# First attention steps in pairs: joint sums, reciprocals and split values, and a bank of its own for the second product

## The chip, the core and the metric

The kernel runs on one core of a Trainium2 chip. The core has five engines that run side by side, each in its own program order: TensorE (PE in the profile, with its weight loads as PEld), VectorE (DVE), ScalarE (ACT), GpSimd (POOL) and SyncE (SP), which issues most of the transfers. [...] TensorE writes into eight banks of PSUM; VectorE and ScalarE read from there. The metric is the device time of one execution in microseconds; it is 542.4 us before the change.

## The reference

Attention with a window, then two feed-forward blocks, condensed here. Only keys within 96 positions back, and the first 8, count:

```python
    scores = scale * np.matmul(q, k.transpose(0, 1, 3, 2))   # 2 x 8 heads, 768 x 768
    bias = -slopes[:, None, None] * dist[None, :, :]
    scores = np.where(keep, scores + bias, -1000000000.0)
    a = np.exp(scores - np.max(scores, axis=-1, keepdims=True))
    a = a / (np.sum(a, axis=-1, keepdims=True) + 1e-09)
    x = np.matmul(a, v)                       # then 1536 rows of 512
    h = x @ w_in                              # 512 -> 2048
    g = np.where(h > 0.0, h, np.exp(np.minimum(h, 0.0)) - 1.0)
    x = g @ w_out                             # 2048 -> 512
    return np.maximum(np.maximum(x @ w1, x @ w2), x @ w3) @ w_out2
```

## The kernel before

The attention is cut into 48 steps. A step is one block of 128 queries for one pair of heads; two steps in a row (even, odd) share one load of queries and keys and one of values, and four pairs make the eight heads of 256 rows. A block's key window has 232 columns (two chunks of 116), or 128 in the first block of a sequence, so of steps 0 to 7 the even ones are narrow and the odd ones wide, and steps 8 to 15 are all wide.

One step goes through the engines so:

- `scores_pe`: TensorE multiplies queries and keys of two heads (L228), into banks S0 and S1 for even steps, y0 and y1 for odd ones;
- `scores_dve`: VectorE adds the distances and takes the extreme of each row (L254), for one head and then the other;
- `scores_act`: ScalarE takes the exponential and its row sums (L275), twice; `sums` adds 1e-9 to the sums (L237);
- `recip` (L266) and `norm` (L288): VectorE divides;
- `turn_pe`: TensorE transposes the result (L298, L304), into one of three banks; `turn_act`: ScalarE copies it back (L315);
- `values_pe`: TensorE multiplies it with the values (L327), into the same bank; `values_high` (ScalarE, L337) and `values_low` (VectorE, L343) split that into two halves, `xh` and `xl`, which later products use.

The order is written by hand (`tc.manual_schedule`): each engine runs its instructions as the Python code emits them. The program's head, the loop over steps 0 to 15 in `windowed`, emits in turn k: scores of step k, transposes of step k-2, value products of step k-3, then the work on VectorE and ScalarE, ending with sums of k, reciprocal and normalisation of k-1 and the subtraction of k-4. Beside it the first weights are converted (`words`, from step 8 on: ScalarE L458 and L477, VectorE L462, L469 and L482) and idle TensorE time is filled with products that nobody reads (`FILL`, L765). The last two steps also emit the first half of the first block's first product (`f.product(h, ...)`, L677, 256 columns). `begin` and `run` follow: for the first 512 rows, 16 products `h` of the first layer, each followed by its activation (`elu_exp`, `elu_max`) and by its part of four output tiles `y` (`out_high` L708, `out_low` L716), with the other attention steps woven between. The remaining blocks and the second feed-forward block come after that.

Of the kernel before, what the change touches and what calls it, by code (L numbers as in the profile page):

```python
# [12 lines left out]
F32 = mybir.dt.float32  # L13
# [4 lines left out]
AF = mybir.ActivationFunctionType  # L18
ALU = mybir.AluOpType
# [18 lines left out]
GRP = 2 * P  # L38
# [78 lines left out]
class Windowed:  # L117
# [121 lines left out]
    def scores_dve(self, k, early=False, other=-1):  # L239
# [9 lines left out]
        p = pool.tile([P, 512], F32, tag=tag, name="p")  # L249
        m = self.sm.tile([P, 8], F32, tag="m", name="m", bufs=4)  # L250
        b0 = P if i else 0
        for u in range(2):
            o = slice(u * WIN, u * WIN + n)
            nc.vector.tensor_tensor_reduce(  # L254
                out=p[:, o], in0=sp[u], in1=self.base[:, b0:b0 + n],
                scale=2.0 ** -(2 * hp + u + 1) / UNIT, scalar=3e38,
                op0=ALU.add, op1=ALU.min, accum_out=m[:, u:u + 1],
            )
            if u == 0:
                self.recip(other)  # L260
        self.p_t[k] = p, m

    def recip(self, k):
        if k in self.p_t:
            m = self.p_t[k][1]
            self.nc.vector.reciprocal(m[:, 6:8], m[:, 4:6])  # L266

    def scores_act(self, k):
        if k >= len(self.steps):
            return  # L270
        n = self.geom(k)[-1]
        p, m = self.p_t[k]
        for u in range(2):
            o = slice(u * WIN, u * WIN + n)
            self.nc.scalar.activation(  # L275
                p[:, o], p[:, o], AF.Exp, bias=m[:, u:u + 1], scale=-1.0,
                accum_out=m[:, 2 + u:3 + u],
            )

    def norm(self, k):  # L280
        if k not in self.p_t:
            return
        nc = self.nc
        n = self.geom(k)[-1]
        p, m = self.p_t[k]
        for u in range(2):
            o = slice(u * WIN, u * WIN + n)
            nc.vector.tensor_scalar(p[:, o], p[:, o], m[:, 6 + u:7 + u], None, op0=ALU.mult)  # L288

    def turn_pe(self, k, tag="TX"):  # L290
        if k not in self.p_t:
            return
        nc = self.nc
        p, _ = self.p_t.pop(k)
# [104 lines left out]
class Feed:  # L399
# [304 lines left out]
    def out_high(self, y, fc, g, n):  # L704
        w = self.w[fc][:, 1]
        for e in range(NCC):
# [527 lines left out]
def windowed(tc, ctx, io, flag):  # L1234
    nc = tc.nc
    f = Feed(tc, ctx, io)
    own = ctx.enter_context(ExitStack())
    at = Windowed(tc, own, io, f.ps, f.xy, f.wt, f.act)
    at.close = own.close
    with tc.manual_schedule():  # L1240
# [9 lines left out]
        first = BLOCKS[0] // GRP * 8  # L1250
        x = f.split_tiles()
# [24 lines left out]
        for k in range(first):  # L1276
# [168 lines left out]
```

## Time and profile before

| | us |
|---|---|
| median of 3 runs (542.32 to 542.52) | 542.4 |
| the profiled execution, as timed | 542.16 |
| its span, first to last instruction | 540.4 |
| TensorE busy in the span | 530.4 |
| VectorE busy | 394.1 |
| ScalarE busy | 287.9 |

The profile is one execution. Its span leaves 1.76 us of the timed run outside. A line of the timeline is an instruction (or a run of alike ones, with their count) with start, duration, engine and line of the code, what it writes and reads, and, in brackets, for how long its engine stood idle before it and what ended that. Durations of neighbours on VectorE and ScalarE overlap a little. An fp32 product shows as two records, so that x8 is four products; the two heads of a step run side by side.

### The profile page before, as it was taken

Reading aid. Unit: us, or ns where it says so; the run is one execution under the profiler, and the core shown is the slowest. Engines: PE = TensorE matmul, PEld = TensorE weight load, DVE = VectorE, ACT = ScalarE, POOL = GpSimd, SP = SyncE. Lnnn points to the kernel's source line nnn. Section 1 sums busy time; section 2 is a strip of 40 time slices with the busy share of each in tenths; the row PEclk is TensorE's granted clock in tenths of the full one; section 3 lists DMA queues with packets and bytes.
Section 4 is the critical chain, followed back from the end, with each engine's and each line's share of the span. In section 5 each row is a group of like instructions: output and inputs, shape, how many; then the busy total and the mean of one; then the engine's idle time right before and its main releaser. Section 6 shows DMA issues by size and latency. Waiting matters only on the chain.

```text
span 540.4 us, 7753 instructions
## 1 busy us (share of the span) xinstructions
PE 530.4 (98%) x2746; PEld 427.0 (79%) x2746; DVE 394.1 (73%) x830; ACT 287.9 (53%) x650; POOL 82.9 (15%) x89
## 2 busy tenths in 40 slices
PE   8999999999999999999999999999999999999995
PEld 6667787777777888787888888788888888888884
DVE  6999999999845344443567657688886989779883
ACT  5989877888756555554645565551256321224120
POOL 4210000001000000000000044421035410335000
PEclk9999999999999999999999999999999999999999
DMA  8928255442210111000000031330028301776024
GB/s 295 384 93 329 106 194 196 156 161 84 101 44 24 45 44 44 21 19 1 0 2 0 5 118 35 116 131 26 1 87 301 138 1 45 272 287 234 1 81 159
DMA packets 23455, 59.21 MB, mean 110 GB/s; under 512 B 2416, under 2 KB 2416, under 8 KB 23408
## 3 DMA queue, kind: packets, MB, share of 16 engines
q1 hardware_dynamic: 18368, 49.46, 26.2%
q10 hardware_dynamic: 5040, 9.18, 4.5%
q8 instruction: 24, 0.39, 0.3%
q14 instruction: 23, 0.19, 0.1%
HBM read 49.19 MB, written 9.44 MB: 108 GB/s over the span
## 4 chain that ended last, share of the span: by engine, by line
PE 91%; DVE 4%; ACT 3%; DMA 1%; issue 0%; SPq 0%; DVEq 0%; ACTq 0%
PE h L677 26%; PE y L708 16%; PE y L716 8%; PE y L1027 8%; PE y L1121 5%; PE y L677 5%; PE S L1027 4%; PE TX L327 3%; PE TX L304 3%; PE S L228 2%; PE TX L1027 2%; PE S L1121 2%; PE S L677 2%; PE h L1027 2%; PE TX L1121 2%; ACT p L275 1%
## 5 line engine op out<-in xcount | busy, mean ns | idle before, releaser
L677 PE MATMUL h<-xh,w 128*128 128x512 f32 (+1 forms) x432 | 122.1, 387 | 0.1
L708 PE MATMUL y<-gh,w 128*128 128x512 f32 x384 | 98.8, 399 | 0.1
L513 POOL TENSOR_TENSOR w<-wr,w 128x512 fp32r<-128x512 f32 x42 | 62.9, 1508 | 232.6 <-ACT w L512 230.4
L677 PEld LDWEIGHTS h<-xh,w 128*128 128x128 f32 x432 | 80.2, 188 | 17.3 <-DVE e L702 0.6
L708 PEld LDWEIGHTS y<-gh,w 128*128 128x128 f32 x384 | 69.8, 188 | 14.5 <-issue 0.7
L677 PE MATMUL h<-xl,w 128*128 128x512 f32 (+1 forms) x216 | 71.0, 386 | 0.0
L702 DVE SCALAR_TENSOR_TENSOR e<-e,h 128x512 f32<-128x512 f32 x48 | 32.9, 686 | 50.0 <-ACT e L698 50.0
L512 ACT CAST w<-wr 128x512 fp32r<-128x512 f32 x42 | 27.5, 663 | 63.5 <-DVE wr L503 51.2
L697 ACT ACTIVATE e<-h 128x512 f32<-128x512 f32 x48 | 28.7, 598 | 55.7 <-PE h L677 50.9
L275 ACT ACTIVATE p<-p,m 128x232 f32<-128x232 f32 (+1 forms) x96 | 44.8, 470 | 17.5 <-DVE m L254 17.2
L716 PE MATMUL y<-gl,w 128*128 128x512 f32 x192 | 51.6, 391 | 0.0
L503 DVE SCALAR_TENSOR_TENSOR wr<-wr 128x512 uint32<-128x512 uint32 x48 | 44.3, 923 | 7.4 <-ACT wr L495 6.0
L689 DVE TENSOR_TENSOR gl<-e,gh 128x512 fp32r<-128x512 f32 x48 | 33.1, 690 | 19.9 <-ACT gh L684 19.9
L677 PEld LDWEIGHTS h<-xl,w 128*128 128x128 f32 x216 | 40.4, 188 | 8.1 <-issue 0.2
L198 POOL TENSOR_SCALAR raw<-raw,qsc 128x256 f32<-128x256 f32 x24 | 16.7, 698 | 192.3 <-DMA raw<-qk 178.4
L1027 PE MATMUL y<-t,w 128*128 128x512 f32 x180 | 42.7, 389 | 0.0
L716 PEld LDWEIGHTS y<-gl,w 128*128 128x128 f32 x192 | 36.0, 188 | 7.9 <-issue 0.3
L684 ACT CAST gh<-e 128x512 fp32r<-128x512 f32 x48 | 29.6, 617 | 23.5 <-DVE e L702 23.3
L469 DVE SCALAR_TENSOR_TENSOR wr<-wr 128x1024 uint32<-128x1024 uint32 (+1 forms) x37 | 40.2, 1098 | 0.6
L1027 PEld LDWEIGHTS y<-t,w 128*128 128x128 f32 x180 | 33.8, 188 | 7.0
L698 ACT ACTIVATE e<-e 128x512 f32<-128x512 f32 x48 | 30.3, 632 | 1.5
L1037 ACT CAST g<-m 128x512 fp32r<-128x512 f32 x18 | 10.9, 621 | 35.5 <-DVE m L1056 27.4
(155 smaller groups left out, 837.7 us busy)
## 6 DMA issues: line engine op xcount, KB each, us to landing
wr<-wa SPq DMA_DIRECT2D x14, 1024.0 KB, 6.9
wr<-wb SPq DMA_DIRECT2D x24, 512.0 KB, 4.7
v<-v SPq DMA_DIRECT2D x24, 256.0 KB, 2.8
part<-row ACTq DMA_DIRECT2D x24, 256.0 KB, 4.5
raw<-qk SPq DMA_DIRECT2D x16, 312.0 KB, 4.5
row<-part SPq DMA_DIRECT2D x12, 256.0 KB, 3.1
out<-rows ACTq DMA_DIRECT2D x11, 256.0 KB, 2.8
raw<-qk SPq DMA_DIRECT2D x8, 260.0 KB, 4.7
```

Of the source, the lines that this page charges most:

```text
L275: self.nc.scalar.activation(p[:, o], p[:, o], AF.Exp, bias=m[:, u:u + 1], scale=-1.0, accum_out=m[:, 2 + u:3 + u],)
L469: self.nc.vector.scalar_tensor_tensor(r[..., 0], r[..., 1], v, r[..., 0], op0=op, op1=ALU.bitwise_or)
L503: self.nc.vector.scalar_tensor_tensor(t, a, c, t, op0=op, op1=ALU.bitwise_or)
L513: nc.gpsimd.tensor_tensor(w[:, u, 1], v, w[:, u, 0].bitcast(F32), op=ALU.subtract)
L677: nc.tensor.matmul(out[:, o:n], w[:, part % 2, c * P:c * P + P], (xl if part == 2 else xh)[:, c, o:n], start=(c, part) == order[0], stop=( ...
L689: (engine or self.nc.vector).tensor_tensor(gl[:, 0:n], e[:, 0:n], gh[:, 0:n].bitcast(F32), op=ALU.subtract)
L698: self.nc.scalar.activation(e, e, AF.Exp, scale=-1.0)
L702: self.nc.vector.scalar_tensor_tensor(e, e, -1.0, h, op0=ALU.add, op1=ALU.max)
L708: self.nc.tensor.matmul(y[e][:, 0:n], w[:, a, e * P:e * P + P], g[0][:, 0:n], start=fc == 0 and a == 0, stop=False,)
L716: self.nc.tensor.matmul(y[e][:, 0:n], w[:, 0, e * P:e * P + P], g[1][:, 0:n], start=False, stop=fc == NFC - 1,)
L1027: self.nc.tensor.matmul(out, w[:, u, i % 2, b + c * P:b + c * P + P], o[:, i // 2, c], start=c == i == 0, stop=c == 1 and i == 2,)
L1121: nc.tensor.matmul(o, t[:, a, r], w[:, u, b], start=u == k == 0, stop=u == 1 and k == 2,)
```

## The change

Steps 0 to 13 are emitted in pairs. `sums` and `recip` take a count, and the two steps of a pair share one small tile `m`, so that one instruction serves four columns. The values of two steps go into one bank by `pair_pe`, and `pair_high` and `pair_low` split 256 columns at once. The transposes of a pair both stand in the odd turn: the even step's in bank y3, the odd step's in TX or y2 by turns, where the pair's values follow. Steps 6 and 11 take the buffer of tag `e`. Steps 14 and 15 are written out and go step by step, with the two halves of the first product (`part`) in their old number. The second product takes bank y3 and no longer bank h; the first outputs are issued for the first three output tiles, high and low, and then for the fourth.

```diff
-    def sums(self, k):
+    def sums(self, k, n=1):
         if k in self.p_t:
-            m = self.p_t[k][1]
-            self.nc.scalar.activation(m[:, 4:6], m[:, 2:4], AF.Copy, bias=1e-9)
+            _, m, c = self.p_t[k]
+            o = slice(c, c + 2 * n)
+            self.nc.scalar.activation(m[:, 2, o], m[:, 1, o], AF.Copy, bias=1e-9)
...
+    def recip(self, k, n=1):
         if k in self.p_t:
...
+            self.nc.vector.reciprocal(m[:, 3, o], m[:, 2, o])
...
+    def pair_high(self, k, x):
+        if k >= 0:
+            g, hp, _ = self.steps[k]
+            o = slice(g * GRP, g * GRP + GRP)
+            self.nc.scalar.copy(x[0][:, hp, o], self.t_t[k + 1][0][:, 0:GRP])
+
+    def pair_low(self, k, x):
+        if k >= 0:
+            g, hp, _ = self.steps[k]
+            o = slice(g * GRP, g * GRP + GRP)
+            self.t_t.pop(k)
+            self.nc.vector.tensor_tensor(
+                x[1][:, hp, o], self.t_t.pop(k + 1)[0][:, 0:GRP],
+                x[0][:, hp, o].bitcast(F32), op=ALU.subtract,
             )
...
-        h = self.ps.tile([P, 512], F32, tag="h", name="h")
+        h = self.ps.tile([P, 512], F32, tag="y3", name="h")
         self.product(h, self.w[1][:, 0], x, n, order=BEHIND)
...
-        self.out_high(y, 0, prev, n)
-        self.out_low(y, 0, prev, n)
+        for rows in range(NCC - 1), (NCC - 1,):
+            self.out_high(y, 0, prev, n, rows)
+            self.out_low(y, 0, prev, n, rows)
...
-            at.turn_pe(k - 2, tags[k % 3])
-            at.values_pe(k - 3)
-            if k >= first - 2:
-                f.product(h, f.w[0][:, 0], x, GRP, 0, (k - first + 2) * 6, 6)
-            at.scores_dve(k, True)
-            at.turn_act(k - 2, nc.scalar.copy)
-            at.scores_act(k)
-            at.values_high(k - 3, x)
-            at.sums(k)
-            at.recip(k - 1)
-            at.norm(k - 1)
-            at.values_low(k - 4, x)
...
+        for k in range(0, last, 2):
+            ahead(k)
+            at.pair_pe(k - 4)
+            at.scores_dve(k, True, spare=spare)
+            at.recip(k - 2, 2)
+            at.norm(k - 2)
+            at.norm(k - 1)
+            at.scores_act(k)
+            at.pair_high(k - 4, x)
+            behind(k)
+            k += 1
+            ahead(k)
+            at.turn_pe(k - 3, "y3")
+            at.turn_pe(k - 2, ("TX", "y2")[k // 2 % 2])
+            at.scores_dve(k, True, mates=mates, spare=spare)
+            at.scores_act(k)
+            at.sums(k - 1, 2)
+            at.turn_act(k - 3, nc.scalar.copy)
+            at.turn_act(k - 2, nc.scalar.copy)
+            at.pair_low(k - 5, x)
+            behind(k)
...
+        k = last
+        ahead(k)
+        at.pair_pe(k - 4)
+        part(0)
+        at.scores_dve(k, True)
+        at.recip(k - 2, 2)
+        at.norm(k - 2)
+        at.norm(k - 1)
+        at.turn_pe(k - 2, tags[k % 3])
+        at.scores_act(k)
+        at.pair_high(k - 4, x)
+        at.sums(k)
+        at.turn_act(k - 2, nc.scalar.copy)
+        at.pair_low(k - 4, x)
```

Here `ahead(k)` issues the loads and the scores of step k (and fills), `behind(k)` the next piece of weight conversion.

TensorE in the turns of steps 4 and 5, before (L228 scores, into S0/S1 for step 4 and y0/y1 for step 5; L298 and L304 transposes; L327 value products):

```order
L228 MATMUL S0_235<-raw_135 128x128
L228 MATMUL S1_236<-raw_135 128x128
L298 MATMUL y2_239<-ident_126,p_194 128x128 x2
L327 MATMUL TX_211<-p_169,v_146 64x128 x4
L228 MATMUL y0_259<-raw_135 128x232
L228 MATMUL y1_260<-raw_135 128x232
L304 MATMUL y3_263<-ident_126,p_218 116x128 x4
L327 MATMUL y2_239<-p_194,v_179 64x128 x2
```

And in the changed kernel, the same turns (its lines L309 and L315 are the transposes, L338 the value products):

```order
L228 MATMUL S0_224<-raw_135 128x128
L228 MATMUL S1_225<-raw_135 128x128
L338 MATMUL y2_206<-p_155,v_146 64x128 x2
L338 MATMUL y2_206<-p_168,v_146 64x128 x4
L228 MATMUL y0_246<-raw_135 128x232
L228 MATMUL y1_247<-raw_135 128x232
L309 MATMUL y3_250<-ident_126,p_186 128x128 x2
L315 MATMUL TX_253<-ident_126,p_211 116x128 x4
```

The value products of both steps of a pair have moved between the scores of step 4 and those of step 5, and the transposes of steps 2 and 3 behind the latter.

ScalarE in the turns of steps 4 and 5, before (L275 exponentials, L237 sums, L315 copies of the transposes, L337 the split):

```order
L315 COPY p_194<-y2_239 128x256
L275 ACTIVATE p_246,m_247<-p_246,m_247 128x128 x2
L337 CAST xh_143<-TX_211 128x128
L237 ACTIVATE m_247<-m_247 128x2
L315 COPY p_218<-y3_263 116x512
L275 ACTIVATE p_270,m_271<-p_270,m_271 128x232 x2
L337 CAST xh_143<-y2_239 128x128
L237 ACTIVATE m_271<-m_271 128x2
```

And in the changed kernel (L284, L239, L326 and L364):

```order
L284 ACTIVATE p_234,m_235<-p_234,m_235 128x128 x2
L364 CAST xh_143<-y2_206 128x256
L284 ACTIVATE p_258,m_235<-p_258,m_235 128x232 x2
L239 ACTIVATE m_235<-m_235 128x4
L326 COPY p_186<-y3_250 128x256
L326 COPY p_211<-TX_253 116x512
```

Both copies of a pair now stand behind the pair's one sum.

TensorE in the turns of steps 14 and 15, before (L677 is the first product; S0/S1 belong to step 14, y0/y1 to step 15):

```order
L228 MATMUL S0_542<-raw_340 128x232
L228 MATMUL S1_543<-raw_340 128x232
L304 MATMUL y3_546<-ident_126,p_491 116x128 x4
L327 MATMUL y2_512<-p_454,v_403 64x128 x4
L677 MATMUL h_145<-xh_143,w_467 128x256 x6
L228 MATMUL y0_574<-raw_340 128x232
L228 MATMUL y1_575<-raw_340 128x232
L304 MATMUL TX_578<-ident_126,p_521 116x128 x4
L327 MATMUL y3_546<-p_491,v_470 64x128 x4
```

And in the changed kernel (L705 is the first product):

```order
L228 MATMUL S0_504<-raw_319 128x232
L228 MATMUL S1_505<-raw_319 128x232
L338 MATMUL TX_482<-p_395,v_377 64x128 x4
L338 MATMUL TX_482<-p_425,v_377 64x128 x4
L705 MATMUL h_145<-xh_143,w_434 128x256 x6
L315 MATMUL y3_531<-ident_126,p_457 116x128 x4
L228 MATMUL y0_542<-raw_319 128x232
L228 MATMUL y1_543<-raw_319 128x232
L315 MATMUL TX_546<-ident_126,p_487 116x128 x4
L338 MATMUL y3_531<-p_457,v_437 64x128 x4
```

The transposes of step 12 (before: y3, first in the row after the scores) have moved behind the values of steps 10 and 11 and the six products.

## Rows read from the trace of the kernel before

**Rows 1.** The page: busy time by engine, and the chain that ended last by engine

```profile
PE 530.4 (98%) x2746; PEld 427.0 (79%) x2746; DVE 394.1 (73%) x830; ACT 287.9 (53%) x650; POOL 82.9 (15%) x89
...
PE 91%; DVE 4%; ACT 3%; DMA 1%; issue 0%; SPq 0%; DVEq 0%; ACTq 0%
```

**Rows 2.** Busy time by stretch: us from:to, length, engines, TensorE clock, transfers

```profile
6.00:20.00 14.00, 12.52 (x104) 7.90 (x102) 11.50 (x65) 12.31 (x55) 3.14 (x7) 1.00 1.03 396
20.00:33.00 13.00, 11.91 (x102) 8.21 (x99) 12.82 (x47) 12.50 (x43) 3.09 (x5) 1.00 0.78 279
33.00:45.00 12.00, 11.91 (x108) 8.97 (x106) 10.47 (x42) 10.49 (x35) 1.02 (x1) 1.00 0.44 167
45.00:150.00 105.00, 104.85 (x588) 82.88 (x587) 99.17 (x210) 84.69 (x187) 6.31 (x7) 1.00 0.43 154
```

**Rows 3.** The chain that ended last, in order of time: start, us, what

```profile
10.70 0.95 ACT p L275 x4
...
12.73 0.21 DVE xl L343
...
14.32 0.95 ACT p L275 x4
...
17.94 0.95 ACT p L275 x4
```

**Rows 4.** Timeline of steps 0 to 3, ScalarE and VectorE: start, us, engine, what

```profile
6.88 0.39 ACT L275 ACTIVATE p<-p,m 128x128 f32<-128x128 f32 x1
...
7.50 0.47 ACT L275 ACTIVATE p<-p,m 128x232 f32<-128x232 f32 x1
...
7.82 0.48 DVE L288 TENSOR_SCALAR p<-p,m 128x128 f32<-128x128 f32 x2
...
8.56 0.20 ACT L237 ACTIVATE m<-m 128x2 f32<-128x2 f32 x1
...
8.72 0.37 ACT L315 COPY p<-y 128x256 f32<-128x256 f32 x1
8.80 0.17 DVE L266 RECIPROCAL m<-m 128x2 f32<-128x2 f32 x1
...
9.00 0.59 DVE L288 TENSOR_SCALAR p<-p,m 128x232 f32<-128x232 f32 x2
...
9.51 0.39 DVE L254 CUSTOM_DVE_ANT_0 p<-y,rel 128x232 f32<-128x232 f32 x1
...
10.60 0.49 ACT L275 ACTIVATE p<-p,m 128x232 f32<-128x232 f32 x1
```

**Rows 5.** Timeline of steps 5 to 8, TensorE and the reduce that waits for it

```profile
13.63 0.44 PE L327 MATMUL y<-p,v 128*64 128x128 f32 x4
...
14.95 0.66 PE L327 MATMUL y<-p,v 116*64 116x128 f32 x8
...
15.53 0.66 PE L228 MATMUL y<-raw 64*128 64x232 f32 x4
...
17.62 0.66 PE L228 MATMUL S<-raw 64*128 64x232 f32 x4
...
18.31 0.40 DVE L254 CUSTOM_DVE_ANT_0 p<-S,rel 128x232 f32<-128x232 f32 x1 [0.33 <-PE S L228]
```

**Rows 6.** Timeline of the last steps, and the second product's first weight load

```profile
32.54 1.23 DVE L469 SCALAR_TENSOR_TENSOR wr<-wr 128x1024 uint32<-128x1024 uint32 x1
...
33.69 0.39 DVE L254 CUSTOM_DVE_ANT_0 p<-S,rel 128x232 f32<-128x232 f32 x1
...
33.91 0.98 PE L677 MATMUL h<-xh,w 128*128 128x256 f32 x6
...
35.45 0.62 PE L304 MATMUL TX<-ident,p 128*116 128x128 f32 x4
...
36.11 0.58 ACT L315 COPY p<-TX 116x512 f32<-116x512 f32 x1 [0.68 <-PE TX L304]
...
45.36 0.19 PEld L677 LDWEIGHTS h<-xh,w 128*128 128x128 f32 x1 [0.35 <-DVE e L702]
```

More of the change, by code (lines that the diff above doesn't have):

```diff
@@ L232, in scores_pe, with scores_dve @@
             self.s_t[s] = [x[:, o:o + n] for x in sp]
-    def sums(self, k):
+    def sums(self, k, n=1):
         if k in self.p_t:
-            m = self.p_t[k][1]
-            self.nc.scalar.activation(m[:, 4:6], m[:, 2:4], AF.Copy, bias=1e-9)
-    def scores_dve(self, k, early=False, other=-1):
+            _, m, c = self.p_t[k]
+            o = slice(c, c + 2 * n)
+            self.nc.scalar.activation(m[:, 2, o], m[:, 1, o], AF.Copy, bias=1e-9)
+    def scores_dve(self, k, early=False, other=-1, mates=(), spare=()):
         if k not in self.s_t:
@@ L248, in scores_dve @@
         pool, tag = (self.act, "gh") if early and k % 4 > 1 else (self.sm, "p")
-        p = pool.tile([P, 512], F32, tag=tag, name="p")
-        m = self.sm.tile([P, 8], F32, tag="m", name="m", bufs=4)
+        if k in spare:
+            p = self.act.tile([P, 512], F32, tag="e", name="p", bufs=1)
+        else:
+            p = pool.tile([P, 512], F32, tag=tag, name="p")
+        if k - 1 in mates:
+            m, c = self.p_t[k - 1][1], 2
+        else:
+            m, c = self.sm.tile([P, 4, 4], F32, tag="m", name="m", bufs=4), 0
         b0 = P if i else 0
@@ L256, in scores_dve @@
                 scale=2.0 ** -(2 * hp + u + 1) / UNIT, scalar=3e38,
-                op0=ALU.add, op1=ALU.min, accum_out=m[:, u:u + 1],
+                op0=ALU.add, op1=ALU.min, accum_out=m[:, 0, c + u:c + u + 1],
             )
@@ L260, in scores_dve @@
                 self.recip(other)
-        self.p_t[k] = p, m
-    def recip(self, k):
+        self.p_t[k] = p, m, c
+    def recip(self, k, n=1):
         if k in self.p_t:
-            m = self.p_t[k][1]
-            self.nc.vector.reciprocal(m[:, 6:8], m[:, 4:6])
+            _, m, c = self.p_t[k]
+            o = slice(c, c + 2 * n)
+            self.nc.vector.reciprocal(m[:, 3, o], m[:, 2, o])
     def scores_act(self, k):
@@ L271, in scores_act @@
         n = self.geom(k)[-1]
-        p, m = self.p_t[k]
+        p, m, c = self.p_t[k]
         for u in range(2):
@@ L275, in scores_act @@
             self.nc.scalar.activation(
-                p[:, o], p[:, o], AF.Exp, bias=m[:, u:u + 1], scale=-1.0,
-                accum_out=m[:, 2 + u:3 + u],
+                p[:, o], p[:, o], AF.Exp, bias=m[:, 0, c + u:c + u + 1], scale=-1.0,
+                accum_out=m[:, 1, c + u:c + u + 1],
             )
@@ L284, in norm @@
         n = self.geom(k)[-1]
-        p, m = self.p_t[k]
+        p, m, c = self.p_t[k]
         for u in range(2):
             o = slice(u * WIN, u * WIN + n)
-            nc.vector.tensor_scalar(p[:, o], p[:, o], m[:, 6 + u:7 + u], None, op0=ALU.mult)
+            nc.vector.tensor_scalar(
+                p[:, o], p[:, o], m[:, 3, c + u:c + u + 1], None, op0=ALU.mult
+            )
     def turn_pe(self, k, tag="TX"):
@@ L293, in turn_pe @@
         nc = self.nc
-        p, _ = self.p_t.pop(k)
+        p = self.p_t.pop(k)[0]
         tp = self.ps.tile([P, 512], F32, tag=tag, name=tag)
@@ L345, in values_low @@
                 x[0][:, hp, o:o + P].bitcast(F32), op=ALU.subtract,
+            )
+    def pair_high(self, k, x):
[11 more added lines that the diff above has]
+                x[0][:, hp, o].bitcast(F32), op=ALU.subtract,
             )
@@ L702, in elu_max, with out_high @@
         self.nc.vector.scalar_tensor_tensor(e, e, -1.0, h, op0=ALU.add, op1=ALU.max)
-    def out_high(self, y, fc, g, n):
+    def out_high(self, y, fc, g, n, rows=range(NCC)):
         w = self.w[fc][:, 1]
-        for e in range(NCC):
+        for e in rows:
             for a in range(2):
@@ L711, in out_high, with out_low @@
                 )
-    def out_low(self, y, fc, g, n):
+    def out_low(self, y, fc, g, n, rows=range(NCC)):
         w = self.w[fc][:, 1]
-        for e in range(NCC):
+        for e in rows:
             self.nc.tensor.matmul(
@@ L1275, in windowed, with ahead @@
         tags = "TX", "y2", "y3"
-        for k in range(first):
+        last = first - 2
+        mates, spare = range(0, last, 2), (6, 11)
+        def ahead(k):
             e = k % 2
@@ L1284, in windowed, with behind @@
                 f.fill(at.ident, FILL[k])
-            at.turn_pe(k - 2, tags[k % 3])
-            at.values_pe(k - 3)
-            if k >= first - 2:
-                f.product(h, f.w[0][:, 0], x, GRP, 0, (k - first + 2) * 6, 6)
-            at.scores_dve(k, True)
-            at.turn_act(k - 2, nc.scalar.copy)
-            at.scores_act(k)
-            at.values_high(k - 3, x)
-            at.sums(k)
-            at.recip(k - 1)
-            at.norm(k - 1)
-            at.values_low(k - 4, x)
+        def behind(k):
             if k >= CONV:
@@ L1300, in windowed, with part @@
                 f.w_load()
+        for k in range(0, last, 2):
[19 more added lines that the diff above has]
+            behind(k)
+        def part(n):
+            f.product(h, f.w[0][:, 0], x, GRP, 0, n * 6, 6)
+        k = last
[12 more added lines that the diff above has]
+        at.pair_low(k - 4, x)
+        behind(k)
+        k += 1
+        ahead(k)
+        at.turn_pe(k - 2, tags[k % 3])
+        at.values_pe(k - 3)
+        part(1)
+        at.scores_dve(k, True)
+        at.turn_act(k - 2, nc.scalar.copy)
+        at.scores_act(k)
+        at.values_high(k - 3, x)
+        at.sums(k)
+        at.recip(k - 1)
+        at.norm(k - 1)
+        behind(k)
         def half(first, count):
```

## The prediction

> **What bounds the kernel now.** I read the page first: TensorE is busy for 98% of the span and holds 91% of the chain that ended last [rows 1]. By that, little can be won. But the share is an average, so I next cut the span into stretches [rows 2]. From 45 us on TensorE is busy for 104.85 of 105 us: whatever comes late there ends late, one to one. Before 45 us it is another program, the first 16 attention steps. From 6 to 20 us ScalarE is busy for 88% and VectorE for 82%; neither is full, so a loop of waits sets the pace. From 20 to 33 us VectorE is busy for 12.82 of 13 us: it is the bound. From 33 to 45 us both stand idle for 1.5 us, and the hand-overs decide again. The change edits these three stretches, and each has its own price.
>
> I use short names: S(k) the score products of step k, X(k) its reduce on VectorE (L254), E(k) its two exponentials, T(k) the transposes, C(k) their copy by ScalarE, V(k) the value products.
>
> The chain of waits shows the loop of 6 to 20 us [rows 3]: E of an odd step starts at 10.70, 14.32 and 17.94, so a pair of steps takes 3.62 us. Between two of them stand normalisation, subtraction, T, C. TensorE only steps in with T; S and V are not on the loop.
>
> **The change, part by part.** The order of instructions shows that it does what it says: sums, reciprocals and split values are issued once for two steps, and T of both steps stands behind S of the odd step. Times below are set against the profiled run (540.4 us span, 542.16 us as timed, 0.24 under the median).
>
> *Start.* The sum between E(0) and E(1) goes, so E(1) starts when E(0) lets ScalarE go, 6.88 + 0.39 = 7.27 and not 7.50 [rows 4]. From E(1) to its sum are 8.56 - 7.50 = 1.06 us, to the reciprocal 0.24, to the normalisation 0.20. That of step 0 holds VectorE for 0.40 (0.48 less the 0.08 by which 9.00 + 0.59 passes 9.51), that of step 1 for 0.51. X(3) then takes 0.40 and hands over in 0.02. E(3) starts at 7.27 + 1.06 + 0.24 + 0.20 + 0.40 + 0.51 + 0.42 = 10.10, where it is 10.60 now: 0.50 earlier.
>
> *The loop, steps 3 to 7.* In the new order TensorE has, in one queue, S(even), V of the pair two back, S(odd), T, T. V needs the copies C, and C now stand behind the joint sum on ScalarE. So S(odd) waits behind V, V behind C, C behind the sum, the sum behind E(odd), and E(odd) behind X(odd), which needs S(odd): a closed loop. Its length: sum 0.12 (0.20 less 0.08 overlap), C of 256 columns 0.29 (0.37 less 0.08), C of 512 columns 0.58 [rows 4, 6], hand-over 0.05 (estimate; 17.62 + 0.66 to 18.31 is 0.03 [rows 5]), V 0.80, S to X 0.69, X to E 0.42, E to sum 1.06. V: two products take 0.44, four 0.66, so six 0.88, and the next group starts 0.08 before their end (15.53 against 14.95 + 0.66); S to X is 17.62 to 18.31, a start on which VectorE waited [rows 5]. Sum: 4.01 us, 0.39 over today's 3.62. Two turns cost 0.78, so E(7) starts at 10.10 + 8.02 = 18.12 and not at 17.84.
>
> *Into the second stretch.* X(8) needs S(8), which now stands behind S(7), T(6), T(7). S(7) started at 18.12 - 0.42 - 0.69 = 17.01; then 0.58, 0.33 (two transposes, between nothing and the 0.54 of four, put at four less the value products' step of 0.11 each), 0.54 and 0.69: X(8) at 19.15 and not at 18.31 [rows 5, 6]. **+0.84.**
>
> *VectorE-bound, X(8) to X(14).* Three pairs each lose one reciprocal (0.20, 8.80 to 9.00) and have one subtraction of 256 columns for two of 128 (0.21 each [rows 3]). No row has the wide one: it costs between 0.21 and 0.42, I take 0.32. So 0.30 a pair, 0.20 to 0.41. **-0.90** (0.6 to 1.2). X(14) then comes within 0.1 us of today's 33.69.
>
> *The way out, X(14) to C(13).* Today C(13) starts at 36.11, 2.42 after X(14) [rows 6]. In the new order T(12) and T(13) wait for a normalisation issued only after X(14), and on TensorE they stand behind V(10), V(11) and six products of the first block (and T(13) behind S(15) too). V(10) needs the copies behind the joint sum: from X(13) 0.42 + 1.06 + 0.12 + 0.50 + 0.58 + 0.05 = 2.73, while X(14) stands at X(13) + 0.64 + 0.32 + 1.15 (two heads, the subtraction, the weight conversion of 32.54 to 33.69) = 2.11. So V starts 0.62 after X(14). Then V 1.02, the six products 0.90 (0.98 less 0.08), T(12) 0.54, S(15) 0.58, T(13) 0.62 and 0.04 to the copy: 4.32. Against 2.42 that is **+1.90**. From C(13) on ScalarE has the same order in both kernels, so nothing there earns it back unless idle time takes it up.
>
> *Second product's bank.* The second product has its own bank, so it no longer waits for the activation to be read from the first's: TensorE's weight load stood idle for 0.35 before it [rows 6]. About 0.05 of that is the usual switch. **-0.30**, between 0 and -0.35. The first outputs by rows put the one that reuses this bank behind nine products of the others; I cost it at nothing because these nine cover the activation's read of that bank, and at up to 0.3, the size of the wait removed, if that read is late. The removed instructions on ScalarE (one sum per pair, 0.12) cost and bring nothing of their own where the loop above decides. Transfers keep their order on SyncE; a load that waits for V to free its buffer moves with V, by under 1 us, and is used four pairs later, which covers that. The spare buffers of steps 6 and 11 cost nothing: the pair's V, ahead of X in time, frees the others.
>
> Sum: 0.84 - 0.90 + 1.90 - 0.30 = **+1.54 us**. On the profiled run 543.7, on the median 542.4 + 1.5 = **543.9**. Ends of the unknown terms: 0.84 - 0.2 - 1.2 + 1.8 - 0.35 = +0.9, and 0.84 + 0.2 - 0.6 + 2.0 = +2.4: 543.3 to 544.8 for this case.
>
> **Rivals.**
> A, *the joint work pays, faster.* The loop closes through V only because TensorE gets to X(odd) late. Copies end 0.99 after the sum starts, and S(odd) has delivered 0.05 + 0.80 + 0.69 later, at 2.53; VectorE is ready for X(odd) at 0.24 + 0.20 + 0.40 + 0.51 = 1.35. If V and S took under 0.36 us instead of 1.49, ScalarE's own work would set the turn: E 4 x 0.39 to 0.47, some 1.72, copies 0.87, the split 0.29, the sum 0.12: 3.00. Two turns then save 2.0, and V(10), V(11) out of the way of T(12) another 1.02: 1.54 - 3.02 = -1.48, **540.9**. For it speaks VectorE's full stretch; against it the V and S rows, four times too long. [...]
>
> B, *idle time takes up the late copy.* From 33 to 45 us ScalarE stands idle for 12 - 10.49 = 1.51 us [rows 2]. If the 1.90 ate all of it, the sum is about 0: **542.4**. Against it: ScalarE's idle is spent waiting for T, which come late by the same amount.
>
> C, *TensorE's clock falls.* TensorE was granted full clock in every stretch while busy for 89% from 6 to 20 us [rows 2]. In the new loop its groups hold 0.58 + 0.80 + 0.58 + 0.33 + 0.54 = 2.83 of 4.01 us, 71%, with one idle piece of over 1 us a turn. Were the clock to fall to its lower level, V and S on the loop (1.49) would at most double: 3.0 for two turns, **546.9**. [...]
>
> **How the numbers follow.** Forecast 0.72, A 0.08, B 0.12, C 0.08. The range must leave out no more than A and C: from B with 0.2 of room, 542.2, to just above the forecast's upper end, 545.0. About 0.2% (1.08 us) is what a measurement of this kernel can tell from no change. A is faster: 0.08. B, and the 0.10 of the forecast that lies under 543.5, are the same: 0.22. The rest of the forecast and C are slower: 0.70.
>
> **What would show it.** In the changed kernel's trace: E of steps 3, 5 and 7 about 4.0 us apart, the first at 10.1; X(odd) waiting for TensorE; V starting right behind a 512-column copy and S(odd) right behind V. X(8) to X(14) in about 14.5 us, where it is 15.38. C(13) more than 4 us after X(14). The first 512-column product near 46.9, where it is 45.36, with no wait on the activation. The forecast is wrong if the turns are 3.6 us or less, or if C(13) follows X(14) within 3 us; a granted clock under 1.00 before 45 us would mean C.

## The result, and the profile after

The changed kernel takes **546.4 us** (median of six, 544.4 to 546.9) against 542.5 us (542.2 to 542.6): a ratio of 1.0066, 95% interval 1.0056 to 1.0077. It is slower, by 3.9 us in the medians (3.6 in the means, from which the ratio comes), where the forecast was +1.5 us and the range ended at 545.0. Two slow executions of the kernel before, at 660.9 and 1065.7 us, count in none of the numbers below.

The profiled execution took 546.78 us with a span of 544.8 us. The first thing to look at is the clock column of the stretches, which answers to [rows 2]. Busy time by stretch in the changed kernel (from:to, length, then TensorE, its weight loads, VectorE, ScalarE, GpSimd, then TensorE's granted clock, transfers, GB/s):

```profile
10.00:15.00 5.00, 3.47 (x30) 2.58 (x30) 3.25 (x19) 3.52 (x13) 0.87 (x2) 0.90 1.03 407
15.00:20.00 5.00, 4.53 (x27) 3.00 (x26) 2.35 (x13) 2.96 (x13) 0.96 (x2) 0.50 1.04 397
20.00:25.00 5.00, 5.00 (x40) 3.58 (x40) 4.06 (x19) 4.97 (x16) 0.47 (x1) 0.92 0.69 229
```

In the kernel before, the clock is 1.00 from 6 to 150 us. Here it is 0.50 from 15 to 20 us, a level that the trace of the kernel before shows only behind its last product (at 533.8), from 537.9 us on; the single instructions put the low stretch at 13.7 to 20.6 us. TensorE looks busier in it (4.53 of 5 us) because its instructions take longer (V 1.55 us instead of 0.88, below). That was rival C.

The chain of the changed kernel, which answers to [rows 3], shows a turn of the loop on either side of the fall (start, length, what):

```profile
10.48 1.06 ACT p L284 x4
...
12.57 0.88 PE y L338 x12
13.45 0.64 PE y L228 x4
14.63 1.06 ACT p L284 x4
...
16.71 1.55 PE TX L338 x12
18.26 1.08 PE y L228 x4
```

V (L338) and S of the odd step (L228) now lie on the chain, which they did not before. The turn E(3) to E(5) takes 14.63 - 10.48 = 4.15 us. In the next one V takes 1.55 instead of 0.88 and S 1.08 instead of 0.64, and E(7) comes 5.29 us after E(5).

The timeline has the four places on which the rest hangs: the first value products of a pair, X(8), X(14) and C(13). They answer to [rows 5, 6]:

```profile
12.57 0.88 PE L338 MATMUL y<-p,v 128*64 128x128 f32 x12 [1.53 <-ACT p L326]
...
21.45 0.40 DVE L262 CUSTOM_DVE_ANT_0 p<-S,rel 128x232 f32<-128x232 f32 x1 [0.90 <-PE S L228]
...
36.02 0.40 DVE L262 CUSTOM_DVE_ANT_0 p<-S,rel 128x232 f32<-128x232 f32 x1
...
40.38 0.58 ACT L326 COPY p<-TX 116x512 f32<-116x512 f32 x1 [0.59 <-PE TX L315]
```

The first row is the pause: TensorE stood still for 1.53 us until the second copy C was done, and 1.15 us later its clock fell. X(8) is 3.14 us later than before (18.31), X(14) 2.33 us later (33.69), C(13) 4.27 us later (36.11). Of each, 0.37 us is a later X(0) (6.51 against 6.14), a scatter that the last section takes up. From there on the distance changes little: the second block's first product is 4.1 us later (56.90 against 52.78) and the last product of the kernel 4.5 us (538.3 against 533.8); what adds the last 0.4 us was not followed up.

The weight loads of the second product and of the first outputs (the bracket is idle time and what ended it):

```profile
49.27 0.19 PEld L705 LDWEIGHTS h<-xh,w 128*128 128x128 f32 x1
...
55.50 0.30 PEld L736 LDWEIGHTS y<-gh,w 128*128 128x128 f32 x2 [0.34 <-DVE e L730]
```

The wait of 0.35 us ahead of the second product [rows 6] is gone, and a wait of 0.34 us on the same kind of read now stands ahead of the fourth output row.

### The profile page after: what moved, and what is told of

Same layout as the page of the kernel before. It is cut to its first block, busy times and chain, and to the rows that moved or that the text cites. A ratio compares the mean times of both kernels' runs of the same rounds, so it can differ in the third digit from the quotient of the medians.

```text
span 544.8 us, 7720 instructions
## 1 busy us (share of the span) xinstructions
PE 532.7 (98%) x2746; PEld 429.3 (79%) x2746; DVE 392.8 (72%) x817; ACT 287.8 (53%) x637; POOL 81.6 (15%) x89
## 4 chain that ended last, share of the span: by engine, by line
PE 92%; ACT 3%; DVE 3%; DMA 1%; issue 1%; SPq 0%; ACTq 0%; DVEq 0%
PE h L705 27%; PE y L736 16%; PE y L744 8%; PE y L1056 7%; PE y L1150 4%; PE y L705 4%; PE S L1056 4%; PE TX L338 3%; PE TX L315 3%; PE S L228 3%; PE S L1150 2%; PE TX L1056 2%; PE S L705 2%; PE h L1056 2%; PE TX L1150 1%; ACT p L284 1%
## 5 line engine op out<-in xcount | busy, mean ns | idle before, releaser
L705 PE MATMUL h<-xh,w 128*128 128x512 f32 (+1 forms) x432 | 122.2, 387 | 0.0
L705 PEld LDWEIGHTS h<-xh,w 128*128 128x128 f32 x432 | 80.1, 188 | 17.4 <-issue 0.5
L705 PE MATMUL h<-xl,w 128*128 128x512 f32 (+1 forms) x216 | 71.0, 386 | 0.0
L284 ACT ACTIVATE p<-p,m 128x232 f32<-128x232 f32 (+1 forms) x96 | 44.8, 470 | 21.8 <-DVE m L262 21.7
L705 PEld LDWEIGHTS h<-xl,w 128*128 128x128 f32 x216 | 40.4, 188 | 8.2 <-issue 0.2
```

The source lines that it names most:

```text
L284: self.nc.scalar.activation(p[:, o], p[:, o], AF.Exp, bias=m[:, 0, c + u:c + u + 1], scale=-1.0, accum_out=m[:, 1, c + u:c + u + 1],)
L705: nc.tensor.matmul(out[:, o:n], w[:, part % 2, c * P:c * P + P], (xl if part == 2 else xh)[:, c, o:n], start=(c, part) == order[0], stop=( ...
```

## The experiments

All are compared with the kernel before on the same chip, whose median was 542.3 to 542.6 us. e1, e2, e3 and e5 ran on one chip, e4, e6, e7 and e8 on a second, e9 to e11 on a third, so that across these groups the ratio is the better comparison.

| label | edit | median us | ratio to before, 95% |
|---|---|---|---|
| e8_after | the changed kernel again | 545.6 | 1.0057 (1.0044 to 1.0069) |
| e1_fills | more empty products at three pauses | 544.6 | 1.0039 (1.0025 to 1.0052) |
| e7_one_piece | more empty products at one pause | 544.7 | 1.0040 (1.0027 to 1.0053) |
| e6_nofill | before, without its empty products | 543.1 | 1.0021 (1.0003 to 1.0038) |
| e3_loop | e1, V later in two turns | 543.7 | 1.0023 (1.0013 to 1.0033) |
| e4_out | e1, pairs for steps 0 to 7 only | 543.7 | 1.0024 (1.0015 to 1.0034) |
| e5_loop_out | both of these | 542.5 | 1.0004 (0.9994 to 1.0013) |
| e9_tail | e1, T(12) and T(13) ahead | 544.4 | 1.0036 (1.0023 to 1.0050) |
| e10_late_all | e1, V later in all turns | 547.3 | 1.0089 (1.0073 to 1.0104) |
| e2_bank | before, with the bank and the rows | 542.3 | 0.9999 (0.9990 to 1.0008) |
| e11_no_rows | e2 without the rows | 543.1 | 1.0018 (1.0009 to 1.0027) |

### The clock: e1, e8, e7

The kernel has a table FILL of empty products (L793), which work on nothing that is used later. e1 adds some at the pauses of the paired loop:

```diff
-FILL = {1: 2, 2: 2, 8: 2, 9: 2, 10: 2, 11: 2, 12: 2, 13: 2}
+FILL = {1: 2, 2: 4, 4: 4, 6: 4, 8: 2, 9: 2, 10: 2, 11: 2, 12: 2, 13: 2}
```

> The changed kernel, with the empty products of L793 raised where TensorE idles in the paired loop: 4 instead of 2 behind S(2), and 4 new ones each behind S(4) and S(6). Nothing else differs. Theory 1 (the lower TensorE clock costs about 2.0 to 2.4 us of the loss, on top of a loss of 1.5 to 2 us by the order alone): the granted clock is 1.00 in 10:15, 15:20 and 20:25, the turn E(5) to E(7) falls from 5.29 to about 4.1 us, and the time is 544.3 us (543.8 to 544.8). Theory 2 (the clock comes out of the loop's stalls and is not their cause; the loss is in the order): the time stays within 0.5 us of 546.4. Theory 3 (the added products stand in the way of V or S of the next turn): clock 1.00 but a turn of over 4.6 us and 545.5 us or more.

Measured: 544.6 us, the five from 544.0 to 545.0. The stretches and the same places of e1:

```profile
10.00:15.00 5.00, 4.56 (x42) 3.38 (x42) 3.25 (x19) 3.59 (x14) 0.81 (x2) 1.00 1.03 408
15.00:20.00 5.00, 4.64 (x42) 3.37 (x40) 3.37 (x18) 3.97 (x18) 0.48 (x1) 1.00 1.04 398
20.00:25.00 5.00, 4.16 (x36) 2.88 (x34) 4.69 (x17) 4.94 (x16) 1.02 (x2) 1.00 0.90 317
```

```profile
12.51 0.88 PE L338 MATMUL y<-p,v 128*64 128x128 f32 x12 [0.44 <-ACT p L326]
...
19.55 0.40 DVE L262 CUSTOM_DVE_ANT_0 p<-S,rel 128x232 f32<-128x232 f32 x1 [0.22 <-PE S L228]
...
22.41 0.40 DVE L262 CUSTOM_DVE_ANT_0 p<-y,rel 128x232 f32<-128x232 f32 x1 [0.27 <-PE y L228]
...
34.54 0.39 DVE L262 CUSTOM_DVE_ANT_0 p<-S,rel 128x232 f32<-128x232 f32 x1
...
38.89 0.59 ACT L326 COPY p<-TX 116x512 f32<-116x512 f32 x1 [0.59 <-PE TX L315]
```

The pause ahead of V shrinks from 1.53 to 0.44 us, the clock stays at 1.00, and V starts after E(3) as it did: the empty products delay nothing. E(5) and E(7) come 4.15 and 4.14 us after their forerunners (ScalarE's timeline below), X(8) at 19.55. So more work on TensorE, of no use for the result, makes the kernel faster by 1.8 us against the first six executions. The empty products shorten the pauses and raise the busy share at once; no run here tells the two apart.

```profile
10.41 0.49 ACT L284 ACTIVATE p<-p,m 128x232 f32<-128x232 f32 x1 [0.81 <-DVE m L262]
...
14.56 0.49 ACT L284 ACTIVATE p<-p,m 128x232 f32<-128x232 f32 x1 [0.76 <-DVE m L262]
...
18.70 0.49 ACT L284 ACTIVATE p<-p,m 128x232 f32<-128x232 f32 x1 [0.76 <-DVE m L262]
```

Not every pause brings a fall. e1 has a long one left, ahead of V(10,11), and its granted clock is 1.00 from 33 to 45 us all the same:

```profile
35.24 1.09 PE L338 MATMUL TX<-p,v 116*64 116x128 f32 x16 [1.20 <-ACT p L326]
```

e8 is the changed kernel, unaltered:

> The changed kernel itself, unaltered, beside the others of this call. Expected: the granted clock at 0.50 for some us between 13 and 21 us in most executions, and 546.3 us (544.4 to 547); an execution without the fall comes in near the 544.6 us of the kernel with added empty products.

Measured: 545.6 us, six from 544.95 to 546.4. The fall came at another moment in the profiled execution. TensorE's timeline in it:

```profile
12.18 1.55 PE L338 MATMUL y<-p,v 128*64 128x128 f32 x12 [1.53 <-ACT p L326]
...
17.48 0.88 PE L338 MATMUL TX<-p,v 128*64 128x128 f32 x12 [1.10 <-ACT p L326]
```

Here the low stretch begins right behind the pause, at 12.2, and ends at 15.4: V(0,1) is slow and V(2,3) is not. The price is 0.96 us over e1 by the medians; the twelve executions of the changed kernel spread over 2.5 us, the five of e1 over 1.0. One of the twelve, at 544.4 us, had a mean clock of 0.998, within the 0.997 to 0.999 of e1; eight had 0.990 to 0.995, which no execution of the kernel before has (0.996 to 0.999); the other three, at 0.996 and 0.997, took 544.95 to 545.7 us, and the mean clock alone does not say whether it fell in them.

e7 covers one pause of the three:

```diff
-FILL = {1: 2, 2: 2, 8: 2, 9: 2, 10: 2, 11: 2, 12: 2, 13: 2}
+FILL = {1: 2, 2: 2, 4: 4, 8: 2, 9: 2, 10: 2, 11: 2, 12: 2, 13: 2}
```

> The changed kernel with 4 empty products behind S(4) alone, in the idle piece of 1.53 us ahead of V(0,1), the last long one before the clock fell at 13.72 us. The idle pieces behind S(2) and S(6) stay as in the changed kernel. Theory 1 (that one piece sets the clock off): 1.00 in 10:15 and 15:20, 544.6 us (544.0 to 545.1), as with all three pieces filled. Theory 2 (it is the pauses of all turns together): the clock still falls, later, behind the pause ahead of V(2,3) at about 16.7 us, and the time lies between, at 545 to 546.4 us. Theory 3 (the fall does not come from these pauses): 546.4 us.

Measured: 544.7 us, between theories 1 and 2. Three of the six have a mean clock of 0.998 or 0.999 and take 544.3 to 544.7 us; the profiled one fell. Its stretches:

```profile
10.00:15.00 5.00, 4.42 (x40) 3.14 (x38) 3.20 (x19) 3.94 (x15) 0.75 (x2) 1.00 1.03 409
15.00:20.00 5.00, 3.70 (x26) 2.56 (x26) 2.63 (x14) 3.97 (x17) 0.48 (x1) 0.78 1.04 397
```

The first pause is covered and 10 to 15 us stays at 1.00; the next pause, left as it was, then brings the fall from 17.8 us on. So no single pause does it: the fall came behind the one ahead of V(0,1) in the two profiles of the changed kernel and behind the one ahead of V(2,3) here.

### The same clock in the kernel before: e6

```diff
-FILL = {1: 2, 2: 2, 8: 2, 9: 2, 10: 2, 11: 2, 12: 2, 13: 2}
+FILL = {}
```

> The kernel before without any of the empty products of the loop (steps 1, 2 and 8 to 13; the ones at the very start stay). All else is the same. Theory 1 (pauses of TensorE in this stage cost clock in this kernel too): the granted clock falls to 0.50 for some us between 6 and 36 us. Where it falls behind 20 us, VectorE is the bound and hides most of it: 542.5 to 543.5 us; where it falls in 10 to 20 us, the loop turn stretches as in the changed kernel: 544 us or more. Theory 2 (the empty products do nothing here): the clock stays at 1.00 and the time is 542.5 us, within 0.3.

Measured: 543.1 us with a wide spread, 542.1 to 547.1. The stretches of its profiled execution (545.6 us):

```profile
5.00:8.00 3.00, 2.42 (x15) 1.67 (x14) 2.47 (x12) 1.20 (x6) 1.15 (x2) 1.00 1.01 359
8.00:10.00 2.00, 1.44 (x7) 0.82 (x8) 1.93 (x11) 1.79 (x9) 0.76 (x2) 0.92 1.03 407
10.00:15.00 5.00, 5.00 (x27) 2.88 (x27) 2.67 (x16) 3.84 (x18) 0.78 (x2) 0.50 1.02 408
...
25.00:33.00 8.00, 6.26 (x48) 4.03 (x47) 7.89 (x28) 7.92 (x28) 1.54 (x2) 0.82 0.60 194
33.00:45.00 12.00, 11.91 (x96) 8.15 (x94) 9.84 (x40) 8.40 (x30) 1.29 (x2) 0.83 0.26 81
```

Without them the old order loses its clock too, from just before 10 to 16.5 us and again from about 30 to 37 us. The idle time ahead of the first fall is shorter than the one pause of 1.53 us in the changed kernel: from 5 to 10 us TensorE stands still for 1.14 us in all (0.58 up to 8 us and 0.56 behind it). From 25 to 33 us, where the second fall begins, it is 1.74 us in all; how long the single pauses were is not shown. Of its twelve executions, five with a mean clock of 0.998 or more take 542.1 to 543.2 us and five at 0.982 to 0.988 take 544.8 to 547.1. The other two, at 0.993 and 0.991, take 543.0 and 542.5 us: a fall can also cost little or nothing. Where it lay in these no trace shows; that it lay where VectorE is the bound is only argued.

### The loop and the way out: e3, e4, e5

These three keep the added empty products, so that the clock is 1.00 from 10 to 45 us in the profiled execution of each. e3 moves V of a pair behind the odd step's scores, in the turns of steps 4 and 6 (its split moves with it, behind the odd step's E):

```diff
         for k in range(0, last, 2):
+            late = k in (4, 6)
             ahead(k)
-            at.pair_pe(k - 4)
+            if not late:
+                at.pair_pe(k - 4)
...
             ahead(k)
+            if late:
+                at.pair_pe(k - 5)
             at.turn_pe(k - 3, "y3")
```

> The kernel of e1 (added empty products), with V of the steps 0 to 3 moved in the turns of steps 4 and 6: pair (0,1) and pair (2,3) are multiplied behind S(5) and S(7) instead of behind S(4) and S(6), and their split copy stands behind E(5) and E(7). This takes the chain C to V to S(odd) to X(odd) out of two loop turns. Theory 1 (the joint order of the loop loses because V of a pair stands ahead of the odd step's scores and waits for the second copy): the turns E(3)-E(5) and E(5)-E(7) fall from about 4.1 to about 3.0 to 3.7 us, X(8) comes 1 to 1.4 us earlier, about 0.9 us of it reach the end: 543.4 us (542.9 to 543.9). Theory 2 (VectorE bounds from step 8 on whatever comes before): X(8) earlier, but C(13) moves by less than 0.3 us: 544.1 or more.

e4 and e5 end the pairs early: e4 with the loop as changed, e5 with that of e3. Behind step 8, which hands over as step 14 did, steps 9 to 15 have the old order.

```diff
-        last = first - 2
+        last = 8
```

> The kernel with added empty products and V of a pair ahead of the odd step's scores, as in the changed kernel, but with pairs for the steps 0 to 7 only; from step 8 on one step at a time. With the three kernels measured before it makes a square: loop as changed or with V moved, and a late or an early end of the pairs. Theory 1 (the two losses stand apart and add up): X(14) to C(13) returns to about 2.4 us and X(8) to X(14) to about 15.4, and it is 1.0 to 1.3 us faster than 544.6, at 543.3 to 543.6 us. Theory 2 (they overlap: what the loop loses is what VectorE then lacks): within 0.5 us of 544.6, since X(8) comes late and the single steps behind it cost VectorE 0.9 us more.

> The kernel of e3, with pairs for the steps 0 to 7 only: from step 8 on sums, reciprocals, normalisations, splits and transposes stand one step at a time, as in the kernel before, with one turn between the two orders. Theory 1 (the way out of pairs, X(14) to C(13) 4.32 instead of 2.42 us, costs more than the joint work saves behind step 8): X(8) to X(14) returns to about 15.4 us, X(14) to C(13) to about 2.4, and the time is 542.5 us (542.1 to 543.0), level with before. Theory 2 (joint work pays and the way out is not what loses): it is slower than e3 by 0.3 us or more.

Measured: 543.7 (e3), 543.7 (e4) and 542.5 us (e5), against 544.6 of e1: theory 1 in all three, though e4 is 0.1 us above its range. X(8) and X(14) in e3, and its C(13):

```profile
18.67 0.39 DVE L262 CUSTOM_DVE_ANT_0 p<-S,rel 128x232 f32<-128x232 f32 x1
...
33.40 0.39 DVE L262 CUSTOM_DVE_ANT_0 p<-S,rel 128x232 f32<-128x232 f32 x1
...
37.74 0.58 ACT L326 COPY p<-TX 116x512 f32<-116x512 f32 x1 [0.59 <-PE TX L315]
```

X(8), X(14) in e4, and its C(13):

```profile
19.57 0.40 DVE L262 CUSTOM_DVE_ANT_0 p<-S,rel 128x232 f32<-128x232 f32 x1 [0.23 <-PE S L228]
...
35.72 0.39 DVE L262 CUSTOM_DVE_ANT_0 p<-S,rel 128x232 f32<-128x232 f32 x1
...
38.15 0.59 ACT L326 COPY p<-TX 116x512 f32<-116x512 f32 x1 [0.68 <-PE TX L315]
```

X(14) and C(13) in e5:

```profile
34.73 0.39 DVE L262 CUSTOM_DVE_ANT_0 p<-S,rel 128x232 f32<-128x232 f32 x1
...
37.16 0.58 ACT L326 COPY p<-TX 116x512 f32<-116x512 f32 x1 [0.69 <-PE TX L315]
```

X(14) to C(13) is 2.43 us in e4 and e5, and 4.35 and 4.34 us in e1 and e3 (33.40 to 37.74 there): whether the pairs run to the end makes 1.9 us, in either loop. X(8) to X(14) is 16.15 and 15.53 us without pairs behind step 8, 14.99 and 14.73 us with them: there the joint work does pay. In medians, moving V is worth 0.9 us (e1 to e3) and 1.2 us (e4 to e5); ending the pairs early is worth 0.9 us (e1 to e4) and 1.2 us (e3 to e5), each within about 0.6 us. Rows tell it more finely. The chain's row of the second block's first product in before, e1, e3, e4 and e5, in this order:

```profile
52.78 2.74 PE h L677 x12
55.41 2.73 PE h L705 x12
54.26 2.76 PE h L705 x12
54.67 2.77 PE h L705 x12
53.68 2.73 PE h L705 x12
```

Counted from X(0) (6.14, 6.44, 6.10, 6.44 and 6.38 us) it comes at 46.64, 48.97, 48.16, 48.23 and 47.30 us: moving V is worth 0.81 and 0.93 us, ending the pairs early 0.74 and 0.86. So the two losses stand apart, and with both edits, and the clock held, the time is level with before within its interval; the rows still have e5 0.66 us behind. It is not faster.

Moving V does not undo all that the loop loses. The turns of e3 fall to 3.20 and 3.72 us (E at 10.07, 13.27 and 16.99), yet X(8) stands 12.57 us behind X(0) in e3 and 12.82 in e5, against 13.11 in e1 and 12.17 before: only 0.5 us won in e3, where 1 to 1.4 were expected. VectorE's timeline in e5 shows what takes the rest back; e3 has the same wait at 18.33:

```profile
18.85 0.42 DVE L371 TENSOR_TENSOR xl<-TX,xh 128x256 fp32r<-128x256 f32 x1 [1.06 <-ACT xh L364]
```

The split that moved with V stands right ahead of X(8), and VectorE waits there for ScalarE's copy of the pair's high part.

### Two cures that move the symptom: e9, e10

e9 takes T(13) out from behind V(10,11), the half product and S(15), without touching the pairs:

```diff
         at.pair_pe(k - 4)
-        part(0)
         at.scores_dve(k, True)
...
         at.norm(k - 1)
-        at.turn_pe(k - 2, tags[k % 3])
+        at.turn_pe(k - 2, "y3")
+        at.turn_pe(k - 1, "y2")
...
         k += 1
         ahead(k)
-        at.turn_pe(k - 2, tags[k % 3])
+        part(0)
         at.values_pe(k - 3)
         part(1)
```

> The kernel with added empty products (544.6 us), with the way out of the pairs in another order: T(12) and T(13) both ahead of S(15) and of the first half of the first product, C(12) and C(13) one behind the other. Theory 1 (T(13) behind V(10,11), the half product, T(12) and S(15) is the whole loss of the way out): C(13) comes about 1.5 us earlier and so does all behind it: 543.0 us (542.6 to 543.4). Theory 2 (the pair that ends late has put V and the first product's first half late as well; what is moved ahead only pushes these back): C(13) 1.5 us earlier, E(15) about 1 us earlier, but T(14), behind the half product moved back, makes E(16) and the second half product gain less than 0.3 us: 544.4 us (544.0 to 544.9).

Measured: 544.4 us, theory 2. ScalarE's timeline in e9 has both copies from 36.60 on and E(16) at 43.38:

```profile
36.60 1.07 ACT L326 COPY p<-y 116x512 f32<-116x512 f32 x2
...
43.38 0.49 ACT L284 ACTIVATE p<-p,m 128x232 f32<-128x232 f32 x1
```

And E(16) in e1:

```profile
43.73 0.49 ACT L284 ACTIVATE p<-p,m 128x232 f32<-128x232 f32 x1
```

Counted from X(0) (6.09 us here, 6.44 in e1), C(13), the second of the two, starts about 1.5 us earlier than in e1, as the full gain wants it. But the half product that gave way now stands ahead of V(12) and T(14), and E(16) starts 37.29 us behind X(0) in both kernels. The second block's first product follows 48.96 and 48.97 us behind X(0). All of the gain is taken back within three steps.

e10 moves V behind the odd step's scores in every turn, not in two, and the split with it:

```diff
             ahead(k)
-            at.pair_pe(k - 4)
             at.scores_dve(k, True, spare=spare)
...
             ahead(k)
+            at.pair_pe(k - 5)
             at.turn_pe(k - 3, "y3")
```

> The kernel with added empty products, with V of a pair behind the odd step's scores in every turn and not in the turns of steps 4 and 6 alone (that one: 543.7 us). Theory 1 (V ahead of the odd step's scores loses in every turn): at or below 543.7 us, X(8) to X(14) below 14.7 us. Theory 2 (from step 8 on VectorE is the bound and the later split of a pair stands in its way): X(8) to X(14) above 15.5 us, and 544.5 us or more.

Measured: 547.3 us, theory 2. VectorE's timeline in e10:

```profile
23.30 0.42 DVE L371 TENSOR_TENSOR xl<-y,xh 128x256 fp32r<-128x256 f32 x1 [1.05 <-ACT xh L364]
...
29.68 0.42 DVE L371 TENSOR_TENSOR xl<-TX,xh 128x256 fp32r<-128x256 f32 x1 [1.05 <-ACT xh L364]
...
35.44 0.42 DVE L371 TENSOR_TENSOR xl<-y,xh 128x256 fp32r<-128x256 f32 x1 [1.11 <-ACT xh L364]
```

From step 8 on VectorE is the bound, and each late split keeps it waiting for over 1 us, until ScalarE has copied the pair's high part (L364): X(8) to X(14) grows to 18.1 us. The same move that gains 0.9 us in the loop loses here. The clock fell in this one too, behind a pause of 2.89 us ahead of V(10,11): it is 0.86 over 33 to 45 us, and V(10,11), from 36.53 on, takes 1.51 us where it takes 1.09 in e1. X(14) starts at 37.05, so the 18.1 us stand almost wholly at full clock, but the 547.3 us hold both losses.

### The bank and the rows: e2, e11

e2 is the kernel before with the third part of the change alone; e11 has the first line of this edit but not the rest:

```diff
-        h = self.ps.tile([P, 512], F32, tag="h", name="h")
+        h = self.ps.tile([P, 512], F32, tag="y3", name="h")
...
-        self.out_high(y, 0, prev, n)
-        self.out_low(y, 0, prev, n)
+        for rows in range(NCC - 1), (NCC - 1,):
+            self.out_high(y, 0, prev, n, rows)
+            self.out_low(y, 0, prev, n, rows)
```

> The kernel before, with only the third part of the change: the second product's accumulator in bank y3 and the first outputs issued as three rows and then the fourth. Theory 1: the wait for the activation of 0.35 us ahead of the first 512-wide product goes (C(13) to it falls by about 0.3 us), and the fourth output row waits up to 0.35 us for elu_max's read of the y3 bank in exchange: 542.2 to 542.6 us, same. Theory 2: the rows cost nothing and the bank pays in full: 542.0 to 542.1, faster by 0.3 to 0.5 us. Theory 3: the rows cost more than the bank gives (the products of the fourth row stand apart and their weights are not covered): 542.8 or more.

> The kernel before with the second product's accumulator in bank y3, but the first outputs issued in the old order, all four rows of the high part and then all four of the low part (with rows split: 542.3 us). Theory 1 (the fourth row's high products wait for elu_max's read of bank y3): the wait grows from about 0.33 us to about 1.0 us, since the three low products no longer stand ahead of it: 542.8 to 543.2 us. Theory 2 (the order of rows does not matter): 542.3 us, the wait 0.4 us or less.

Measured: 542.3 us (e2), level with before, and 543.1 us (e11). The weight loads of e2, with the second product's first and the fourth output row's:

```profile
44.91 0.19 PEld L677 LDWEIGHTS h<-xh,w 128*128 128x128 f32 x1
...
51.13 0.30 PEld L708 LDWEIGHTS y<-gh,w 128*128 128x128 f32 x2 [0.33 <-DVE e L702]
```

And of e11:

```profile
51.40 0.30 PEld L708 LDWEIGHTS y<-gh,w 128*128 128x128 f32 x2 [1.04 <-DVE e L702]
```

The wait has moved, not gone: 0.35 us ahead of the second product become 0.33 us ahead of the fourth row, of which 0.2 us is lost (the first outputs take 52.10 - 48.96 = 3.14 us up to the next T, where they took 52.34 - 49.40 = 2.94). The order by rows is what keeps it at 0.33: without it the wait is 1.04 us.

## Why the prediction was wrong

**The step that failed is the choice between the forecast and rival C.** The forecast assumed full clock and gave C a chance of 0.08. Yet the working had the signs of C in it: 71% busy in the loop and an idle piece of over 1 us a turn. Both came true (3.47 of 5 us is 69%, a part of it at the lower clock already; 1.53 us). Against C it had only that the trace of before has full clock up to 150 us [rows 2], but that loop has no such pause. This is the longest one in it, in TensorE's timeline:

```profile
13.08 0.62 PE L304 MATMUL y<-ident,p 128*116 128x128 f32 x4 [0.66 <-DVE xl L343]
```

That the kernel carries empty products at steps 1, 2 and 8 to 13 stood in the code and was not weighed; e6 shows the clock without them, 0.50 from 10 to 15 us. A pause alone does not tell: the clock fell to 0.50 behind the one of 1.53 us in the changed kernel, while e1 kept 1.00 across 1.20 us. C's price was put at +3.0 us, as if V and S took twice as long in both turns. The doubling was an upper bound; at 0.50 V took 1.55 us instead of 0.88 and S 1.08 instead of 0.64, 1.76 and 1.69 times as long. The profiled fall of after hit one and a half turns: E(5) to X(8) takes 6.82 us, against 4.99 in e1, so 1.8 us. Of these VectorE's stage takes back 0.4 (14.57 against 14.99), which leaves 1.4 us of the medians' 1.8. That C's 546.9 lies within 0.5 us of the measured 546.4 is in part luck: its price was over 1 us too high, and the sum that it was added to 0.6 us too low.

**The rest of the sum, read where the clock is held (e1).**

| term | forecast | measured | |
|---|---|---|---|
| E(3) behind X(0) | 3.96 | 3.97 | held |
| turn of the loop | 4.01 | 4.15, 4.14 | held, 0.13 short each |
| E(7) to X(8) | 1.03 | 0.85 | 0.18 too long |
| X(8) to X(14) | -0.90 | -0.39 | **mis-sized** |
| X(14) to C(13) | 4.32 | 4.35 | held |
| bank and rows | -0.30 | -0.15 | half |

The forecast for E(3) is 10.10 with X(0) at 6.14, as in before; e1 has 10.41 with X(0) at 6.44.

X(8) to X(14): the price per pair was right, but the stretch was not. X(9) in e1 still waits for TensorE (0.27 us, at 22.41), so X(8) to X(9) takes 2.86 us instead of 2.47. From X(9) to X(14) it is 12.13 instead of 12.91 us: 0.78 us saved in two and a half pairs, 0.31 a pair, where I had 0.30. The bound passes to VectorE one step later than I drew the line. The wide subtraction starts the next instruction 0.34 us later, where I took 0.32.

Bank: the gain of 0.3 us is there, but the nine products do not cover the activation's read. I had named 0.3 as the price if that read is late, and taken nothing; it is 0.2. What is left, 0.15 us, is too little for the medians to show (e2: 0.9999, 0.9990 to 1.0008).

Put together for full clock and X(0) at 6.14: 19.25 - 18.31 = 0.94 for X(8), then -0.39, +1.93 and -0.15, so +2.3 us. e1 measures +2.1. The forecast of +1.5 would have been 0.6 us short even without the fall; e1's 544.6 lies just inside the range.

**The rivals.** A fell: in the changed kernel and in e1 no turn went below 4.1 us. What it needed, V off the loop, is e3, with turns of 3.20 and 3.72 us where A had 3.00; even there the late split and the way out remained. B fell: the 1.92 us by which C(13) follows X(14) more late are not taken up by ScalarE's idle time. e3 and e5 differ by 0.58 us at C(13) (37.74 and 37.16) and by 0.58 us at the second block's first product (54.26 and 53.68).

## What to carry to other kernels

Joining work of two steps paid here only on the engine that is the bound: it saved 0.31 us a pair from step 9 on, while in the loop before and on the way out it lengthened a chain of hand-overs, 0.5 us a turn and 1.9 us once. Where a new order makes TensorE stand still in every turn, price a lower clock as a likely case and not as the accident, for here at least eight of twelve executions lost the full one, and two profiles showed 0.50 in its place: put empty products into the pauses first, and then compare orders. Before taking one wait away, look for the next reader of the same bank: here the wait of 0.35 us came back there as one of 0.33 us.

## What the runs showed of the hardware

The moment of the fall is not fixed by the program: with the same instructions the low stretch was 13.7 to 20.6 us in one execution and 12.2 to 15.4 in another, and one of twelve, by its time and mean clock, showed none. With this the changed kernel spreads over 2.5 us, where the kernel before, on any one chip, spreads over 1.0 to 1.4. Nor does the length of a pause settle it: full clock was kept across 1.20 us in e1 and lost in e6, where all idle time from 5 to 10 us makes 1.14 us.

Two scatters of 0.3 to 0.7 us have nothing to do with the change. X(0) starts at 6.09 to 6.14 us in six of the thirteen profiled executions and at 6.38 to 6.51 in seven, in both orders of the loop. From the start of the kernel's last product to the end of the span it takes 5.9 to 6.6 us. Both must be taken off before one profiled execution is set against another to a tenth of a us.
